# Half of the columns between two DFT stages kept in SBUF, moved by GpSimd-issued transfers, in a fused FFT filter and gated FFN kernel

## The chip, the cores and the metric

The kernel runs on one core of one Trainium2 chip. The metric is the device time of one execution in microseconds. Before the change three runs gave 1575.16 us in the median (1572.47 to 1579.84).

## The reference

`x` is 8 x 3136 x 256 in float32. Along the sequence of 3136 it is filtered in the frequency domain; the result goes through a feed-forward block with a gate.

```
X = np.fft.rfft(x, axis=1)
y = np.fft.irfft(X * (filt_r + 1j * filt_i), n=3136, axis=1)     # 8 x 3136 x 256
h = np.maximum(y @ w_in, 0)                                      # 256 -> 1024
conv = conv_w[0] * h[s - 1] + conv_w[1] * h[s] + conv_w[2] * h[s + 1]
out = (h * sigmoid(conv)) @ w_out                                # 1024 -> 256
```

The filter and the FFN weights come as constants too; the weights are 64-bit floats, which the kernel turns into float32 on VectorE.

## The kernel before, in words

The program has two phases. In the first, all eight batches go through the transform; in the second the FFN runs over chunks of 896 positions with TensorE full all the time, and the last stage of the transform of batches 1 to 7 is slipped in between. The change is in the first phase.

The length 3136 is split into 112 x 28. A batch then is 28 columns of 112 points (x 256 channels), worked through in 14 pairs. Each pair takes these steps:

- `first` (L317): TensorE multiplies two columns by `s1_sb` (matmuls at L321); ScalarE copies the result from PSUM into the tile `sa` (L309) and stores it to `a_dram` in DRAM (L315). Rows of a column are 112 outputs, which are 4 groups `r` of 28.
- load `a` (L304): the next stage needs, for an index `g`, the 4 groups of all 28 columns. So it needs the whole batch: 112 rows `(n r)` of `a_dram`, two values of `g` at a time. The way through DRAM is a transposition.
- `second` (L324): one matmul by `s2_sb` (L328; for the last pair L331 with `s2s_sb`).
- `filt` (L334): VectorE makes `u` and two halves of `v` from PSUM and the filter parts `t1_sb` and `t2_sb` (L340, L341, L342), GpSimd adds them to `z` (L344).
- `third` (L347): matmuls with `i1_sb` (L351), copied by ScalarE to `sb` (L309) and stored to `b_dram` (L315). The last stage later reads it as `br` (L199), multiplies by `m2_sb` (L216) and writes `y` (L146, L149).

One loop (L369) over `i` sets the order of the work on TensorE, VectorE, ScalarE and GpSimd by hand: the iteration `i` makes `first` of pair `i - 1`, and, `SKEW` = 18 iterations later, `second` of pair `m - 1`, `filt` of `m - 2` and `third` of `m - 4`, with `m = i - SKEW`. On TensorE a full iteration is thus `third`, `first`, `second`. Two kinds of small work are slipped into it: the conversion of weights (`convert_weights` L273, eight pieces of 11 steps each, one step in eight of nine iterations), and `copy_filter` (L251) on ScalarE, which copies the filter parts to the other partition half. From `done` = 118 on, the last stage of batch 0 runs in the loop as well (L408 to L414). SyncE's queue, which holds all loads, is not ordered by hand: a scheduler orders it. ScalarE's queue holds its own stores in order with its copies. Every transfer of SyncE and ScalarE signals through one of eight semaphores and waits for the transfer that used it before.

Buffers: eight tiles of `x`, five of `a`, four of `sa`, four of `sb`, five of PSUM `ps`, three of PSUM `pp`, three of `z`.

Of the kernel before, what the change touches and what calls it, by code (L numbers as in the profile page):

```python
# [9 lines left out]
F32 = mybir.dt.float32  # L10
# [28 lines left out]
def _dft_tables():  # L39
# [85 lines left out]
def tile_fft_filter_gated_ffn(  # L125
# [56 lines left out]
    a_dram = [dram.tile([N2, 112, D], F32, name=f"a_dram{b}") for b in range(B)]  # L182
# [44 lines left out]
    s1_sb = xp.tile([112, N2, 112], F32, name="s1_sb", bufs=1)  # L227
    with (
# [13 lines left out]
        t2_sb = fc.tile([120, G, D], F32, name="t2_sb")  # L242

        rows = {}

        def load_filter(c):
            sl = slice(4 * c, 4 * c + 4)
            for t, src in ((t1_sb, fr), (t2_sb, fi)):
                nc.sync.dma_start(out=t[0:64, sl], in_=src[:, sl])

        def copy_filter(c):  # L251
            sl = slice(4 * c, 4 * c + 4)
            nc.scalar.activation(t1_sb[64:120, sl], t1_sb[0:56, sl], AF.Copy)
            nc.scalar.activation(t2_sb[64:120, sl], t2_sb[0:56, sl], AF.Copy, scale=-1.0)
            if c == 6:
                nc.sync.dma_start(out=t1_sb[92:93, G - 1], in_=nyq)
# [3 lines left out]
        def load_weights(k):  # L260
            raws[k] = raw = cv.tile([128, 2, 512], I32, name="raw")
            for part, src in enumerate((w_in, w_out)):
                nc.sync.dma_start(out=raw[:, part], in_=src[:, 512 * k:512 * k + 512])

        def convert_conv():
            n = 3 * NF
            raw = cv.tile([128, 2, 512], I32, name="raw")
            nc.sync.dma_start(out=raw[:, 0, 0:2 * n], in_=conv_w)
            yield
            em = cv.tile([128, 2, 512], I32, name="em", bufs=1)  # L270
            yield from to_f32(cw.rearrange("p k f -> p (k f)"), raw[:, 0, 0:2 * n], em[:, 0, 0:n], em[:, 1, 0:n])

        def convert_weights():  # L273

            for k in range(8):
                raw = raws.pop(k)
                em = cv.tile([128, 2, 512], I32, name="em", bufs=1)
                ws = cv.tile([128, 2, 256], F32, name="ws")
                yield from to_f32(ws.rearrange("p t n -> p (t n)"), raw.rearrange("p t n -> p (t n)"), em[:, 0], em[:, 1])
                yield  # L280
                parts = [[t.rearrange("p a b -> p (a b)")[:, 256 * k:256 * k + 256] for t in w] for w in (wi, wo)]
# [6 lines left out]
                if k < 6:  # L288
                    load_weights(k + 2)
# [5 lines left out]
        def pool(kind):  # L295
            return xp if kind in ("x", "sa") else fp

        def load(kind, b, p):
            r = pool(kind).tile([112, 2, D], F32, name=kind, bufs=8 if kind == "x" else 5)
            if kind == "x":  # L300
                v = x[b].rearrange("(p n) d -> p n d", n=N2)
            else:
                v = a_dram[b].rearrange("n (r g) d -> (n r) g d", g=G)
            nc.sync.dma_start(out=r, in_=v[:, 2 * p:2 * p + 2])  # L304
            rows[kind, b, p] = r

        def store(kind, b, p, ps):
            st = pool(kind).tile([112, 2, D], F32, name=kind, bufs=4)
            nc.scalar.activation(st, ps, AF.Copy)  # L309
            sl = slice(2 * p, 2 * p + 2)  # L310
            if kind == "sa":
                v = a_dram[b][sl].rearrange("n p d -> p n d")
            else:
                v = b_dram[b].rearrange("n (r g) d -> (n r) g d", g=G)[:, sl]
            nc.scalar.dma_start(out=v, in_=st)  # L315
# [8 lines left out]
        def second(b, p):  # L324
            r = rows.pop(("a", b, p))
            pp = fps.tile([120, 2, D], F32, name="pp", bufs=3)
            if p < NP - 1:
                nc.tensor.matmul(pp, lhsT=s2_sb, rhs=r, start=True, stop=True)  # L328
            else:
                for j, m in ((0, s2_sb), (1, s2s_sb)):  # L330
                    nc.tensor.matmul(pp[:, j], lhsT=m, rhs=r[:, j], start=True, stop=True)  # L331
            psums[b, p] = pp

        def filt(b, p):  # L334
# [7 lines left out]
            nc.vector.tensor_mul(v[0:56], pp[64:120], t2_sb[64:120, sl])  # L342
# [14 lines left out]
        SKEW = NP + 4  # L357
        nc.sync.dma_start(out=s1_sb[:, 0:4], in_=s1[:, 0:4])
        load("x", 0, 0)
        load("x", 0, 1)  # L360
        for c in range(1, 4):
            nc.sync.dma_start(out=s1_sb[:, 4 * c:4 * c + 4], in_=s1[:, 4 * c:4 * c + 4])
            load("x", 0, 2 * c)
            load("x", 0, 2 * c + 1)
        csteps, wsteps = convert_conv(), convert_weights()
        done = NP * B + 6
        NI = max(NP * B + SKEW + 5, done + N2 // 2 + 3)
        with tc.manual_schedule(engines=COMPUTE):
            for i in range(NI):  # L369
# [5 lines left out]
                if 1 <= i < 4:  # L375
                    nc.sync.dma_start(out=s1_sb[:, 4 * i + 12:4 * i + 16], in_=s1[:, 4 * i + 12:4 * i + 16])
                if (bp := at(f + 7)) and i:
                    load("x", *bp)
                if bp := at(m + 3):
                    load("a", *bp)  # L380
                if i == 6:
                    nc.sync.dma_start(out=s2_sb, in_=s2[:, 0:120])
                    nc.sync.dma_start(out=s2s_sb, in_=s2s[:, 0:120])
# [9 lines left out]
                if bp := at(m - 1):  # L393
                    second(*bp)
                if pt is not None:
                    store("sb", *at(m - 4), pt)
                if pf is not None:
                    store("sa", *at(f - 1), pf)
# [5 lines left out]
                if i >= 22 and i % 9 != 8:  # L404
# [161 lines left out]
```

## Time and profile before

| | |
|---|---|
| profiled execution, span | 1573.9 us |
| runs, median | 1575.16 us |
| TensorE busy over the span | 1510.8 us (96%) |
| VectorE, ScalarE, GpSimd busy | 1280.7, 1192.6, 698.0 us |
| moved by DMA | 166.83 MB, HBM read 88.03, written 77.07 MB |
| DMA from GpSimd's queue | none |

The profile is of one execution. PE is TensorE's matmuls, PEld its weight loads, DVE VectorE, ACT ScalarE, POOL GpSimd, SP SyncE; a trailing q is an engine's issuing of transfers, which does not count as busy. In a group's row stand the line, the engine, the operation and its tiles, how many there were, the busy time in all and the mean of one in ns, and after the second bar how long the engine sat idle ahead of them and what ended that. In a row of windows each engine has its busy time and the number of its instructions, then follow the granted clock of TensorE, the share of the 16 DMA engines that was busy, and the rate.

### The profile page before, as it was taken

The page shows a single profiled execution, that of the slowest core. Times are in us where ns is not written, and L with a number is a line of the kernel's source. Part 1 is how long each engine was busy: PE and PEld are TensorE (multiplying, and loading weights), DVE is VectorE, ACT ScalarE, POOL GpSimd, SP SyncE. Part 2 cuts the span into 40 slices and gives each one's busy share as a digit, 9 for nine tenths or more (in the row PEclk, how much of TensorE's full clock was granted, in tenths as well). Part 3 has the DMA queues.
Part 4 walks back from the last instruction along what each step waited for, and adds up shares of the span by engine and source line. Part 5 has one row for each costly group of instructions (what it writes and reads, how often), then busy time and mean ns, then how long its engine had stood idle before and what let it go on. Part 6 is the DMA issues. An engine that isn't in the chain of part 4 may idle for free.

```text
span 1573.9 us, 26330 instructions
## 1 busy us (share of the span) xinstructions
PE 1510.8 (96%) x9424; PEld 1351.0 (86%) x9424; DVE 1280.7 (81%) x1965; ACT 1192.6 (76%) x2162; POOL 698.0 (44%) x624
## 2 busy tenths in 40 slices
PE   5699999998999999999999999999999999999998
PEld 4366666656999999999999999999999999999998
DVE  0487878897888888888888888888888888888887
ACT  3444444445988888888888888888888888888887
POOL 0255555562444444444444444444444444444444
PEclk8699999999999999999999999999999999999999
DMA  9999999984111011111111111111111111100001
GB/s 292 298 345 349 341 309 338 340 251 142 30 48 48 30 48 48 48 48 48 40 33 36 47 48 49 46 48 47 36 42 48 48 37 41 48 24 25 24 24 48
DMA packets 128278, 166.83 MB, mean 106 GB/s; under 512 B 10682, under 2 KB 87571, under 8 KB 128147
## 3 DMA queue, kind: packets, MB, share of 16 engines
q1 hardware_dynamic: 86931, 113.74, 23.1%
q10 hardware_dynamic: 41216, 51.39, 9.9%
q8 instruction: 75, 1.23, 0.3%
q14 instruction: 56, 0.46, 0.1%
HBM read 88.03 MB, written 77.07 MB: 105 GB/s over the span
## 4 chain that ended last, share of the span: by engine, by line
PE 83%; DMA 9%; DVE 4%; ACT 2%; issue 1%; ACTq 0%; POOL 0%; SPq 0%; DVEq 0%; POOLq 0%
PE ps_h L178 12%; PE ps_h L179 12%; PE ps_h L177 11%; PE po L473 11%; PE po L475 11%; PE po L474 11%; PE ps_h L216 5%; PE ps L321 4%; DMA x<-in_x 3%; PE ps L351 3%; PE pp L328 3%; DMA a<-a_dram 2%; DMA a_dram<-sa 2%; DVE y L149 1%; DVE v L341 1%
## 5 line engine op out<-in xcount | busy, mean ns | idle before, releaser
L152 POOL TENSOR_TENSOR g<-t,g 128x448 fp32r<-128x448 f32 x448 | 517.6, 1156 | 667.6 <-ACT g L146 265.8
L473 PE MATMUL po<-wo,g 128*128 128x256 f32 x1568 | 441.5, 282 | 0.0
L475 PE MATMUL po<-wo,g 128*128 128x256 f32 x1568 | 433.8, 277 | 0.0
L474 PE MATMUL po<-wo,g 128*128 128x256 f32 x1568 | 433.4, 276 | 0.0
L447 DVE SCALAR_TENSOR_TENSOR t<-ps_h,cw,t 128x448 f32<-128x448 f32 x448 | 305.5, 682 | 83.9 <-ACT t L442 73.3
L178 PE MATMUL ps_h<-y,wi 128*128 128x450 f32 x896 | 330.8, 369 | 4.2 <-DVE y L149 4.2
L177 PE MATMUL ps_h<-y,wi 128*128 128x450 f32 x896 | 329.2, 367 | 3.4 <-ACT y L146 2.1
L179 PE MATMUL ps_h<-y,wi 128*128 128x450 f32 x896 | 329.2, 367 | 0.0
L448 DVE SCALAR_TENSOR_TENSOR t<-ps_h,cw,t 128x448 f32<-128x448 f32 x448 | 306.4, 684 | 16.0
L442 ACT ACTIVATE t<-ps_h,cw 128x448 f32<-128x448 f32 x448 | 285.2, 637 | 42.1 <-ACT ps_h L440 0.7
L473 PEld LDWEIGHTS po<-wo,g 128*128 128x128 f32 x1568 | 294.7, 188 | 7.0
L474 PEld LDWEIGHTS po<-wo,g 128*128 128x128 f32 x1568 | 294.3, 188 | 5.7
L475 PEld LDWEIGHTS po<-wo,g 128*128 128x128 f32 x1568 | 294.4, 188 | 0.0
L440 ACT ACTIVATE ps_h<-ps_h 128x450 f32<-128x450 f32 x448 | 251.6, 562 | 32.5 <-PE ps_h L179 27.7
L453 DVE TENSOR_TENSOR t<-ps_h,t 128x448 f32<-128x448 f32 x448 | 275.1, 614 | 0.1
L452 ACT ACTIVATE t<-t 128x448 f32<-128x448 f32 x448 | 255.1, 569 | 12.2 <-DVE t L448 11.0
L146 ACT ACTIVATE g<-t 128x448 fp32r<-128x448 f32 x448 | 254.4, 568 | 0.2 <-DVE t L453 0.2
L344 POOL TENSOR_TENSOR z<-u,v 120x512 f32<-120x512 f32 x112 | 157.2, 1404 | 169.5 <-DVE v L342 144.8
L177 PEld LDWEIGHTS ps_h<-y,wi 128*128 128x128 f32 x896 | 170.4, 190 | 12.0 <-ACT y L146 3.3
L179 PEld LDWEIGHTS ps_h<-y,wi 128*128 128x128 f32 x896 | 168.6, 188 | 13.9
L178 PEld LDWEIGHTS ps_h<-y,wi 128*128 128x128 f32 x896 | 168.6, 188 | 13.5 <-DVE y L149 6.6
L149 DVE TENSOR_TENSOR y<-ps_h,y 128x448 fp32r<-128x448 f32 x98 | 103.1, 1052 | 76.7 <-ACT y L146 76.7
(51 smaller groups left out, 1447.5 us busy)
## 6 DMA issues: line engine op xcount, KB each, us to landing
x<-in_x SPq DMA_DIRECT2D x112, 224.0 KB, 4.6
a_dram<-sa ACTq DMA_DIRECT2D x112, 224.0 KB, 4.5
a<-a_dram SPq DMA_DIRECT2D x112, 224.0 KB, 4.7
b_dram<-sb ACTq DMA_DIRECT2D x112, 224.0 KB, 4.1
br<-b_dram SPq DMA_DIRECT2D x112, 224.0 KB, 2.6
out<-ot SPq DMA_DIRECT2D x27, 896.0 KB, 4.1
raw<-in_w_in SPq DMA_DIRECT2D x8, 256.0 KB, 4.6
raw<-in_w_out SPq DMA_DIRECT2D x8, 256.0 KB, 5.3
```

What stands on the lines that cost most here:

```text
L152: nc.gpsimd.tensor_tensor(out=dst, in0=src, in1=hi.bitcast(F32), op=ALU.subtract)
L177: nc.tensor.matmul(ps, lhsT=wh, rhs=rh, start=start, stop=False, **kw)
L178: nc.tensor.matmul(ps, lhsT=wh, rhs=rl, start=False, stop=False, **kw)
L179: nc.tensor.matmul(ps, lhsT=wl, rhs=rh, start=False, stop=stop, **kw)
L442: nc.scalar.activation(t, h[:, 1:SUB + 1], AF.Copy, scale=cw[:, 1, f:f + 1])
L447: nc.vector.scalar_tensor_tensor(out=t, in0=h[:, 0:SUB], scalar=cw[:, 0, f:f + 1], in1=t, op0=ALU.mult, op1=ALU.add)
L448: nc.vector.scalar_tensor_tensor(out=t, in0=h[:, 2:SUB + 2], scalar=cw[:, 2, f:f + 1], in1=t, op0=ALU.mult, op1=ALU.add)
L452: nc.scalar.activation(t, t, AF.Sigmoid)
L453: nc.vector.tensor_mul(t, h[:, 1:SUB + 1], t)
L473: nc.tensor.matmul(o, lhsT=gh[:, sl], rhs=wo[0][:, f], start=first, stop=False, skip_group_check=True)
L474: nc.tensor.matmul(o, lhsT=gh[:, sl], rhs=wo[1][:, f], start=False, stop=False, skip_group_check=True)
L475: nc.tensor.matmul(o, lhsT=gl[:, sl], rhs=wo[0][:, f], start=False, stop=last, skip_group_check=True)
```

## The change

Of each pair of columns, the even one no longer goes through DRAM. `store_a` writes only the odd column to `a_dram` (now 14 x 112 x 256 for a batch). One iteration later `turn` issues, on GpSimd's queue, a transfer that takes the even column of `sa` (112 rows of 1 KB) to four partitions `p`, `p + 14`, `p + 28`, `p + 42` of a whole-batch buffer `a_sb[b % 2]`, 28 KB in each. The odd columns are loaded into partitions 56 to 111 of it by `load_a`, 112 KB each, two a iteration in the first seven iterations of a batch, from iteration `m + 1` on. `second` reads the buffer. The rows of `s2` are put in the matching order.

To make room for two buffers of 28 KB per partition, other tiles shrink: seven tiles of `x`, three of `sb`; weight pieces of half the size (sixteen of them), two steps an iteration from `i` = 22; `ws` in one buffer; GpSimd's descriptor space at 4096 bytes. `fi` is loaded to partitions 64 to 127 and copied to 0 to 55, where the sign is now taken by VectorE: the third product is a scalar_tensor_tensor with -1.0. The filter is loaded in pieces of 128 KB, twice as many. `SKEW` goes from 18 to 16 and `done` from 118 to 116, so the loop has 133 iterations and not 135.

```diff
-        return np.concatenate([re, gap, im, -im, gap, re], 1)
+        rows = np.array([56 + 2 * (n - 1) + r if n % 2 else 14 * r + n // 2 for n in range(28) for r in range(4)])
...
-    a_dram = [dram.tile([N2, 112, D], F32, name=f"a_dram{b}") for b in range(B)]
+    a_dram = [dram.tile([N2 // 2, 112, D], F32, name=f"a_dram{b}") for b in range(B)]
...
+    a_sb = [xp.tile([112, G, D], F32, name="a_even", bufs=1)]
...
+        a_sb.append(fc.tile([112, G, D], F32, name="a_odd"))
...
-            for k in range(8):
+            for k in range(16):
...
+        def load_a(b, p):
+            v = a_dram[b].rearrange("n (r g) d -> (n r) g d", g=G)
+            nc.sync.dma_start(out=a_sb[b % 2][56:112, 2 * p:2 * p + 2], in_=v[:, 2 * p:2 * p + 2])
+
+        def store_a(b, p, ps):
+            st = xp.tile([112, 2, D], F32, name="sa", bufs=4)
+            nc.scalar.activation(st, ps, AF.Copy)
+            nc.scalar.dma_start(out=a_dram[b][p], in_=st[:, 1])
+            rows["sa", b, p] = st
+
+        def turn(b, p):
+            nc.gpsimd.dma_start(out=a_sb[b % 2][p:56:14], in_=rows.pop(("sa", b, p))[:, 0])
...
-            r = rows.pop(("a", b, p))
+            r = a_sb[b % 2][:, 2 * p:2 * p + 2]
...
-            nc.vector.tensor_mul(v[0:56], pp[64:120], t2_sb[64:120, sl])
+            nc.vector.scalar_tensor_tensor(out=v[0:56], in0=pp[64:120], scalar=-1.0, in1=t2_sb[64:120, sl], op0=ALU.mult, op1=ALU.mult)
...
-        SKEW = NP + 4
+        SKEW = NP + 2
...
-        done = NP * B + 6
+        done = NP * B + 4
...
-                if bp := at(m + 3):
-                    load("a", *bp)
...
+                if bp := at(m + 1):
+                    for p in (2 * bp[1], 2 * bp[1] + 1):
+                        if p < NP:
+                            load_a(bp[0], p)
...
                 if bp := at(m - 1):
                     second(*bp)
+                if bp := at(f - 2):
+                    turn(*bp)
...
-                if i >= 22 and i % 9 != 8:
+                if i >= 22:
+                    next(wsteps, None)
                     next(wsteps, None)
```

GpSimd's instructions around the first converted weights (`ws`, `wi`, `wo` are these, `z` is the sum of the filter), before:

```order
L174 TENSOR_TENSOR ws<-ws,em 128x512
L344 TENSOR_TENSOR z<-u,v_104 120x512
L344 TENSOR_TENSOR z<-u,v_103 120x512
L152 TENSOR_TENSOR wi_81<-ws,wi_80 128x256
L344 TENSOR_TENSOR z<-u,v_104 120x512
L152 TENSOR_TENSOR wo_83<-ws,wo_82 128x256
L344 TENSOR_TENSOR z<-u,v_103 120x512
```

The same place of GpSimd's queue after (`a_odd` is the buffer of batch 1, `sa` the tile that ScalarE filled):

```order
L177 TENSOR_TENSOR ws<-ws,em 128x256
L351 TENSOR_TENSOR z<-u,v_104 120x512
L317 DMA a_odd<-sa 4x28x256
L155 TENSOR_TENSOR wi_81<-ws,wi_80 128x128
L351 TENSOR_TENSOR z<-u,v_105 120x512
L317 DMA a_odd<-sa 4x28x256
L155 TENSOR_TENSOR wo_83<-ws,wo_82 128x128
L351 TENSOR_TENSOR z<-u,v_104 120x512
L317 DMA a_odd<-sa 4x28x256
```

Between any two sums now stands the issue of one transfer.

SyncE's queue at the start of the second stage of batch 1, before (`x` are inputs of `first`, `a` those of `second`):

```order
L304 DMA x<-in_x 112x512
L304 DMA a<-a_dram_58 112x512
L304 DMA x<-in_x 112x512
L304 DMA a<-a_dram_58 112x512
L304 DMA x<-in_x 112x512
L304 DMA a<-a_dram_58 112x512
```

SyncE's queue where the second stage of batch 3 starts, after:

```order
L303 DMA x<-in_x 112x512 x5
L308 DMA a_odd<-a_dram_60 56x512 x9
L303 DMA x<-in_x 112x512
L308 DMA a_odd<-a_dram_60 56x512 x5
L269 DMA raw<-in_w_in 128x256
L269 DMA raw<-in_w_out 128x256
L303 DMA x<-in_x 112x512 x5
```

The loads of the second stage stood one by one between those of `x`; now the fourteen of a batch stand in a block, and the `x` behind them wait in the queue until the first of the block may go.

More of the change, by code (lines that the diff above doesn't have):

```diff
@@ L104, in s2 @@
         re, im, gap = m[:, 0].reshape(112, 56), m[:, 1].reshape(112, 56), np.zeros((112, 8))
-        return np.concatenate([re, gap, im, -im, gap, re], 1)
+        rows = np.array([56 + 2 * (n - 1) + r if n % 2 else 14 * r + n // 2 for n in range(28) for r in range(4)])
+        out = np.zeros((112, 120))
+        out[rows] = np.concatenate([re, gap, im], 1)
+        return out
     i1 = i1.reshape(2, 56, G, 112)
@@ L241, in tile_fft_filter_gated_ffn @@
         t1_sb = fc.tile([120, G, D], F32, name="t1_sb")
-        t2_sb = fc.tile([120, G, D], F32, name="t2_sb")
+        t2_sb = fc.tile([128, G, D], F32, name="t2_sb")
+        a_sb.append(fc.tile([112, G, D], F32, name="a_odd"))
         rows = {}
         def load_filter(c):
-            sl = slice(4 * c, 4 * c + 4)
-            for t, src in ((t1_sb, fr), (t2_sb, fi)):
-                nc.sync.dma_start(out=t[0:64, sl], in_=src[:, sl])
+            for k in range(2):
+                sl = slice(4 * c + 2 * k, 4 * c + 2 * k + 2)
+                nc.sync.dma_start(out=t1_sb[0:64, sl], in_=fr[:, sl])
+                nc.sync.dma_start(out=t2_sb[64:128, sl], in_=fi[:, sl])
         def copy_filter(c):
@@ L287, in convert_weights @@
                     yield
[L288 removed]
+                if k < 14:
                     load_weights(k + 2)
@@ L293, in tile_fft_filter_gated_ffn, with load, store_b @@
         psums = {}
[L295 to L315, printed above, removed]
+        def load(b, p):
+            r = xp.tile([112, 2, D], F32, name="x", bufs=7)
+            nc.sync.dma_start(out=r, in_=x[b].rearrange("(p n) d -> p n d", n=N2)[:, 2 * p:2 * p + 2])
+            rows["x", b, p] = r
+        def load_a(b, p):
[3 more added lines that the diff above has]
+            st = xp.tile([112, 2, D], F32, name="sa", bufs=4)
+            nc.scalar.activation(st, ps, AF.Copy)
+            nc.scalar.dma_start(out=a_dram[b][p], in_=st[:, 1])
+            rows["sa", b, p] = st
+        def turn(b, p):
+            nc.gpsimd.dma_start(out=a_sb[b % 2][p:56:14], in_=rows.pop(("sa", b, p))[:, 0])
+        def store_b(b, p, ps):
+            st = fp.tile([112, 2, D], F32, name="sb", bufs=3)
+            nc.scalar.activation(st, ps, AF.Copy)
+            nc.scalar.dma_start(out=b_dram[b].rearrange("n (r g) d -> (n r) g d", g=G)[:, 2 * p:2 * p + 2], in_=st)
         def first(b, p):
@@ L355, in at @@
             return divmod(i, NP) if 0 <= i < NP * B else None
-        SKEW = NP + 4
+        SKEW = NP + 2
         nc.sync.dma_start(out=s1_sb[:, 0:4], in_=s1[:, 0:4])
-        load("x", 0, 0)
-        load("x", 0, 1)
-        for c in range(1, 4):
+        load(0, 0)
+        load(0, 1)
+        for c in range(1, 3):
             nc.sync.dma_start(out=s1_sb[:, 4 * c:4 * c + 4], in_=s1[:, 4 * c:4 * c + 4])
-            load("x", 0, 2 * c)
-            load("x", 0, 2 * c + 1)
+            load(0, 2 * c)
+            load(0, 2 * c + 1)
+        load(0, 6)
         csteps, wsteps = convert_conv(), convert_weights()
-        done = NP * B + 6
+        done = NP * B + 4
         NI = max(NP * B + SKEW + 5, done + N2 // 2 + 3)
@@ L394, in tile_fft_filter_gated_ffn @@
                     second(*bp)
+                if bp := at(f - 2):
+                    turn(*bp)
                 if pt is not None:
-                    store("sb", *at(m - 4), pt)
+                    store_b(*at(m - 4), pt)
                 if pf is not None:
-                    store("sa", *at(f - 1), pf)
+                    store_a(*at(f - 1), pf)
                 if 3 <= i < 16:
```

30 lines of the change are left out of this document (15 added, 15 removed).

## The prediction

> **What bounds the kernel now.** I read the page's slices first. In its 40 slices of 39.3 us each, the busy tenths of TensorE and of the DMA engines and the moved GB/s are these:
>
> ```profile
> PE   5699999998999999999999999999999999999998
> DMA  9999999984111011111111111111111111100001
> GB/s 292 298 345 349 341 309 338 340 251 142 30 48 48 30 48 48 48 48 48 40 33 36 47 48 49 46 48 47 36 42 48 48 37 41 48 24 25 24 24 48
> ```
>
> The transform is the first ten slices; there the DMA engines are full, later nearly idle. Everything that the change edits lies there. To place the stages I took three matmuls from the chain of waits and the timeline (start, duration): the first `second`, the last `first`, and the first of the last stage of batch 0.
>
> ```profile
> 55.94 2.06 PE pp L328 x2
> ...
> 324.25 1.03 PE L321 MATMUL ps<-x,s_sb 112*112 112x256 f32 x4
> ...
> 342.79 1.04 PE L216 MATMUL ps<-m_sb,br 112*128 112x112 f32 x8
> ```
>
> Cut there, the windows give each engine's busy time and count, the granted clock, the DMA share and GB/s:
>
> ```profile
> core 0: us, PE busy (x) PEld busy (x) DVE busy (x) ACT busy (x) POOL busy (x), PEclk, DMA share, GB/s
> 0.00:56.00 56.00, 29.87 (x89) 19.84 (x89) 5.30 (x13) 20.25 (x29) 4.04 (x10) 0.80 0.98 291
> ...
> 90.00:324.00 234.00, 220.48 (x827) 145.94 (x828) 192.28 (x289) 102.15 (x178) 132.46 (x103) 0.99 1.01 336
> 324.00:343.00 19.00, 15.78 (x55) 8.87 (x53) 18.32 (x28) 6.19 (x12) 12.23 (x9) 1.00 0.76 231
> 343.00:385.00 42.00, 36.36 (x192) 27.15 (x190) 37.51 (x51) 22.79 (x29) 18.63 (x20) 1.00 0.66 195
> 385.00:1573.00 1188.00, 1179.35 (x8176) 1130.95 (x8176) 1005.46 (x1553) 1024.20 (x1893) 518.60 (x476) 1.00 0.13 41
> ```
>
> So: a fill of 56 us (only `first`, DMA share 0.98), a steady stage to 324 us, a drain to 385, and 1189 us of FFN, which I leave as they are. The chain shows what paces the steady stage, in pieces of start, duration and place:
>
> ```profile
> 212.67 0.86 PE ps L321 x4
> 213.54 0.86 PE pp L328 x2
> 214.40 0.86 PE ps L351 x4
> ...
> 216.16 4.54 DMA x<-in_x
> 220.71 5.29 DMA a<-a_dram
> 226.49 0.61 ACT sb L309
> ```
>
> An iteration is 3 x 0.86 = 2.59 us of TensorE while nothing is late; now and then a transfer is. Sizes and landing times of the transfers:
>
> ```profile
> x<-in_x SPq DMA_DIRECT2D x112, 224.0 KB, 4.6
> a_dram<-sa ACTq DMA_DIRECT2D x112, 224.0 KB, 4.5
> a<-a_dram SPq DMA_DIRECT2D x112, 224.0 KB, 4.7
> b_dram<-sb ACTq DMA_DIRECT2D x112, 224.0 KB, 4.1
> br<-b_dram SPq DMA_DIRECT2D x112, 224.0 KB, 2.6
> raw<-in_w_in SPq DMA_DIRECT2D x8, 256.0 KB, 4.6
> t_sb<-in_fr SPq DMA_DIRECT2D x7, 256.0 KB, 5.4
> i_sb<-in_i SPq DMA_DIRECT2D x7, 210.0 KB, 5.2
> s_sb<-in_s SPq DMA_DIRECT2D x7, 196.0 KB, 4.3
> ```
>
> An iteration moves 4 x 224 KB = 917 kB, at 336 GB/s 2.73 us; weights (512 KB per 12.4 iterations, 42 kB each) add 0.13: 2.86 us. The stage makes 82 iterations (82 sums `z` in the rows below) in 234 us, 2.85 us each. DMA sets the pace now, a tenth above TensorE. The rows of VectorE and GpSimd in that window (count, busy us, mean ns, idle before):
>
> ```profile
> L344 POOL TENSOR_TENSOR z<-u,v 120x512 f32<-120x512 f32 x82 | 115.9, 1414 | 92.3 <-DVE v L342 77.5 <-PE pp L328 12.1 <-PE ps L321 2.4
> L342 DVE TENSOR_TENSOR v<-pp,t_sb 56x512 f32<-56x512 f32 x82 | 56.8, 693 | 2.4
> L340 DVE TENSOR_TENSOR u<-pp,t_sb 120x512 f32<-120x512 f32 x81 | 56.0, 692 | 35.9 <-PE pp L328 28.4 <-POOL z L344 5.2 <-issue 0.7
> L341 DVE TENSOR_TENSOR v<-pp,t_sb 56x512 f32<-56x512 f32 x81 | 55.4, 684 | 2.0
> L174 POOL TENSOR_TENSOR ws<-ws,em 128x512 f32<-128x512 f32 x7 | 8.9, 1267 | 0.0
> L152 POOL TENSOR_TENSOR wo<-ws,wo 128x256 fp32r<-128x256 f32 x7 | 5.1, 729 | 0.0
> L152 POOL TENSOR_TENSOR wi<-ws,wi 128x256 fp32r<-128x256 f32 x7 | 5.1, 728 | 11.2 <-ACT wi L146 11.2
> L172 DVE SCALAR_TENSOR_TENSOR em<-raw,em 128x512 f32<-128x512 uint32 x6 | 4.2, 693 | 0.2
> L162 DVE TENSOR_SCALAR em<-raw 128x512 int32<-128x512 int32 x7 | 3.0, 428 | 0.2
> ```
>
> **Steady stage, DMA.** Of 224 KB stored and 224 KB loaded per iteration, 112 KB of each go, and 112 KB of `turn` come: 784 KB = 803 kB, 2.39 us at 336 GB/s, with 48 kB of weights 2.53 us. Below TensorE's 2.59, so the most that is to be had from this is 2.85 - 2.59 = 0.26 us an iteration.
>
> **VectorE.** The scalar_tensor_tensor that replaces the third product costs the same: that form took 693 ns over as many columns (L172), the product 693. A half-size weight piece is seven operations of half the length; with three of 0.69 and four of 0.43 whole, at least 1.9 us per 5.5 iterations. 2.07 + 0.35 = 2.42 us: hidden under 2.59, with little to spare.
>
> **GpSimd.** An iteration is a sum, 1.41 us, and a share of the weights, (1.27 + 0.73 + 0.73) / 2 per 5.5 iterations = 0.25. New is the issue of `turn`, X. No transfer of before is issued by GpSimd, so I bound it: SyncE's issue of one is
>
> ```profile
> 199.82 0.31 SPq L304 DMA_DIRECT2D x<-in_x  x1
> ```
>
> 0.31 us; the upper end is a whole unhurried transfer, 2.6 us (`br`). GpSimd has to write out 112 rows in software where SyncE only hands them over, and its own shortest regular instruction is 0.73 us; I take 1.0, nearer to that row than to either end. At the low end TensorE paces (2.59 us); at the high end the pace would be 4.26 us, and how far towards it is weighed with the first rival. Then GpSimd needs 1.41 + 0.25 + 1.0 = 2.66 us, more than TensorE: it becomes the pace by a hair, and it has to be gap-free. Behind a `turn` in its queue wait the next sums, and `third` two iterations later waits for these. The Trainium skill (DMA: Bandwidth & Descriptors, Latency and other measured facts) puts the first byte of a GpSimd-issued transfer at about 1 us and of a SyncE or ScalarE one at 0.6; if the 0.4 between them were all of the extra work, X would be 0.7 and TensorE would stay the pace.
>
> **Batch boundaries.** Before, `a` was loaded four iterations ahead of its use; now the first `load_a` is issued two ahead, and it waits for the store of the batch's last column. Counted from the start of that column's iteration: `first` done at 1.7, copy and issue to about 2.7, landing 3 to 4.5 (between `br` and `sa`), issue 0.3, landing again 3 to 4.7: 9.0 to 12.2. `second` stands at 3 x 2.59 + 1.7 = 9.5. The last `turn` goes out an iteration after, behind its sum: at 2.6 + 2.1 + 1.4 + X = 7.1, landing 3 to 4.5, 10.1 to 11.6. So `second` is late by nothing to 2.7 us, and what stands behind in TensorE's and SyncE's queues (fourteen loads in a block, then `x`) shifts along; ScalarE's stores share the eight semaphores with that block. That ScalarE can be held by such a load shows in the waits (in total, times, longest):
>
> ```profile
> ACT sb L309 <- DMA a<-a_dram: 24.0, 13, 5.7
> ```
>
> I take 2.5 us for each of the boundaries, 2.5 / 14 = 0.18 us an iteration. Pace: 2.66 + 0.18 = 2.84 us.
>
> **Fill.** `second` now stands at iteration 17, behind all filter loads in SyncE's queue. Ahead of it go, as the queue stands now, in KB: 24 `x` 5376, `s1` 1372, filter 3584, `i1` 1470, the small tables about 180 by their shapes, weights 512, and 16.5 iterations of stores and turns 3696: 16,190 KB = 16.6 MB, at 291 GB/s 57 us. As late as before, but at iteration 17 and not 19.
>
> **Sum.** To the last `first`, 57 + 95 x 2.84 = 327 us (before 324). Drain: the last stage starts 5 and not 7 iterations after it. Those 19 us held 28 VectorE instructions, 24 of the filter and 4 of weights; the weights are done by iteration 110 now, so 5 x 2.2 = 11 us (2.07 of VectorE and its gaps): -8, and one boundary in it, +2.5. Total 3 - 5.5 = -2.5 us: 1571.4 for the span of 1573.9. The median of the runs is 1.3 above that span, so 1572.7: I say 1572. Gain or loss goes with the pace: 95 us for each us of it. Under 0.5% (8 us) a difference is about what the measurement can't tell.
>
> **Rivals.**
> *GpSimd sets the pace* (slower). Above X = 1.03 the sum turns positive; at X = 1.5, 1.41 + 0.25 + 1.5 = 3.16, with half the boundary loss hidden 3.25: 57 + 309 - 324 - 5.5 = +36, 1612; at 1.2, 2.86 and 2.95 to 3.04, +8 to +16. The high end of 2.6 us would make +132, 1707. For: a `turn` in each gap between sums, and the sums are at 1.41 already. Against: GpSimd sat idle 92 us before its 82 sums, 1.13 us each. Chance 0.30.
> *A turn is slow in landing.* Its destination has four rows of 28 KB. If only four of the sixteen engines carry it, each moves 28 KB where `sa` put 14 KB on each in 4.5 us; L could reach 7. ScalarE needs the tile again four iterations after its copy, so and the turn is issued an iteration after that, at 2.1 + 1.4 + 1.0 = 4.5 us of it, the copy at 2.0 of its own: with the pace P, 4P + 2.0 >= P + 4.5 + L, P >= (2.5 + L) / 3 = 3.17, 57 + 301 - 324 - 5.5 = +29, 1604; at L = 5 it is nothing. Chance 0.07. The Trainium skill (DMA: Bandwidth & Descriptors, Why a DMA increments its semaphore by 16 and not by 1) has the engines limited to the largest count up to 16 that divides both slowest dimensions, here 4; no transfer of this trace has such a shape.
> *All is hidden.* X at 0.7, landings near 2.6 us as on unhurried queues, boundaries without loss: P = 2.65, 57 + 252 - 324 - 8 = -23, 1552. For: the DMA engines would have 15% to spare. Against: four engines within a few per cent of one pace, in tight buffers. Chance 0.20.
> *Nothing relieved.* SBUF-to-SBUF bytes could cost DMA engines as much as the two halves that they replace: P stays 2.85, 1572 also. Chance 0.03.
>
> **How the numbers follow.** Forecast 0.40, most within 0.5% of 1575 (0.20), 0.13 better, 0.07 worse. Faster 0.13 + 0.20 = 0.33; same 0.20 + 0.02 (mild slow landing) + 0.03 = 0.25; slower 0.07 + 0.30 + 0.05 = 0.42. Range: down to 1550 (all hidden, 0.07 beyond), up to 1606 (X about 1.45; with slow landing 0.12 beyond). The forecast's own range is 1560 to 1584.
>
> **What would show it.** Right: 2.6 to 2.9 us between sums in the steady stage, DMA share under 0.95, GpSimd with next to no idle time, `second` late once in 14. Wrong: sums over 3 us apart with GpSimd's issues of more than 1.2 us between them; ScalarE waiting for `turn` at `sa`; a drain that is not shorter; a fill far from 57 us.

## The result, and the profile after

The changed kernel takes 1676.20 us in the median of four runs (1671.94 to 1682.61), the kernel before, run beside it, 1576.97 us (1572.47 to 1579.84). The ratio is 1.063, with a 95% interval of 1.060 to 1.066: slower by 99 us, where 1572 was forecast and 1606 was the upper end. The profiled execution of after has a span of 1680.6 us.

The slices of its page (40 of 42.0 us) already show where to look: the FFN is as before, the transform takes twelve slices and not ten, and the DMA engines are nearly full at two thirds of the rate.

```profile
PE   4387877887889999999999999999999999999998
DMA  9878888787631111111111111111101111100001
GB/s 224 194 207 242 223 227 230 225 239 209 182 109 29 50 45 34 45 50 50 45 45 45 34 45 45 50 45 50 45 29 45 50 45 49 46 29 23 23 23 45
```

To cut the time by stage I took from the timeline of TensorE the first `second`, which names what it waited for, of after and of before:

```profile
78.42 2.03 PE L335 MATMUL pp<-a_even,s_sb 112*120 112x512 f32 x2 [13.56 <-DMA a_even<-a_dram]
```

```profile
44.82 2.06 PE L328 MATMUL pp<-a,s_sb 112*120 112x512 f32 x2 [10.06 <-DMA a<-a_dram]
```

Before, this is at 44.8 and not at 55.9. The prediction took the first `second` that stood in the chain of waits for the first that ran. With cuts at the first `second`, the last `first` and the first matmul of the FFN, the windows of after and then of before are these (the columns as in the prediction's windows):

```profile
0.00:78.40 78.40, 25.27 (x68) 15.88 (x69) 1.16 (x7) 10.44 (x17) 11.76 (x23) 0.66 0.91 211
78.40:425.40 347.00, 277.92 (x950) 175.08 (x951) 282.57 (x396) 131.89 (x233) 207.36 (x236) 0.91 0.82 223
425.40:491.10 65.70, 53.28 (x231) 37.32 (x229) 48.40 (x66) 27.41 (x37) 25.95 (x26) 0.89 0.62 174
```

```profile
0.00:44.80 44.80, 23.43 (x76) 16.49 (x76) 1.16 (x7) 16.94 (x25) 1.51 (x8) 0.83 0.97 293
44.80:324.20 279.40, 256.08 (x930) 167.76 (x931) 218.50 (x328) 122.50 (x205) 147.25 (x113) 0.95 1.01 331
324.20:385.10 60.90, 51.94 (x243) 35.85 (x242) 55.64 (x79) 29.04 (x40) 30.67 (x28) 1.00 0.69 206
```

So 34 us more in the fill, 68 in the steady stage (95 iterations of 3.65 us, before 93 of 3.00), 5 in the drain. In the steady stage no engine is full: VectorE is busy 283 of 347 us, GpSimd 207, and DMA fell to 223 GB/s. The issue of a turn on GpSimd, and how long a turn takes to land, by the groups (84 to 424 us) and the page's list of DMA issues:

```profile
L317 POOL DMA_DIRECT2D a_odd<-sa x51 | 35.2, 691 | 29.4 <-ACT sa L312 29.1
L317 POOL DMA_DIRECT2D a_even<-sa x42 | 28.9, 688 | 24.2 <-ACT sa L312 24.1
```

```profile
a_even<-sa POOLq DMA_DIRECT2D x56, 112.0 KB, 6.5
a_odd<-sa POOLq DMA_DIRECT2D x56, 112.0 KB, 6.1
```

A turn costs GpSimd 0.69 us and lands after 6.1 to 6.5 us. The waits (84 to 424 us; total, times, longest) are spread over many pairs, with the transfers around `sa` and the late products of VectorE among them; for a turn itself ScalarE waits little, which is the last two lines, 8.3 us together:

```profile
POOL z L351 <- DVE v L349: 80.8, 45, 6.7
ACT sa L312 <- DMA a_even<-a_dram: 29.3, 3, 11.9
ACT sa L312 <- DMA x<-in_x: 17.6, 10, 6.7
PE pp L335 <- DMA a_even<-a_dram: 12.9, 2, 8.3
ACT sa L312 <- DMA a_even<-sa: 5.1, 3, 2.0
...
ACT sa L312 <- DMA a_odd<-sa: 3.2, 3, 1.3
```

VectorE's timeline shows the two conversion steps of an iteration: the first takes 0.29 or 0.45 us, the second is stretched, and the next `u` starts only behind it. Below it is what GpSimd does at these times.

```profile
250.54 0.29 DVE L173 TENSOR_SCALAR em<-ws 128x256 int32<-128x256 int32 x1
250.87 1.37 DVE L175 SCALAR_TENSOR_TENSOR em<-raw,em 128x256 f32<-128x256 uint32 x1
252.27 0.69 DVE L347 TENSOR_TENSOR u<-pp,t_sb 120x512 f32<-120x512 f32 x1
...
258.73 0.45 DVE L163 TENSOR_SCALAR em<-raw 128x256 int32<-128x256 int32 x1
259.09 2.26 DVE L165 TENSOR_SCALAR em<-raw 128x256 int32<-128x256 int32 x1
```

```profile
250.69 1.27 POOL L351 TENSOR_TENSOR z<-u,v 120x512 f32<-120x512 f32 x1 [2.33 <-DVE v L349]
...
259.10 0.47 POOL L155 TENSOR_TENSOR wi<-ws,wi 128x128 fp32r<-128x128 f32 x1
259.51 0.46 POOL L155 TENSOR_TENSOR wo<-ws,wo 128x128 fp32r<-128x128 f32 x1
259.93 1.27 POOL L351 TENSOR_TENSOR z<-u,v 120x512 f32<-120x512 f32 x1
```

And ScalarE's timeline in the fill shows copies that wait some 10 us each for a load of constants that they have nothing to do with. The likely reason is that the store ahead of them in the queue shares a semaphore with that load.

```profile
36.44 0.60 ACT L312 ACTIVATE sa<-ps 112x512 f32<-112x512 f32 x1 [9.96 <-DMA i_sb<-in_i]
...
48.39 0.60 ACT L312 ACTIVATE sa<-ps 112x512 f32<-112x512 f32 x1 [11.36 <-DMA t_sb<-in_fr]
```

That gave three theories. **A**: VectorE's conversion steps, two in a row under a sum of GpSimd. **B**: the order of SyncE's queue, which a scheduler makes, with the eight semaphores that SyncE and ScalarE share. **C**: a turn is carried by few of the sixteen DMA engines, and what crosses these is slowed.

### The profile page after: what moved, and what is told of

Its sections match the earlier page's. It is cut to its first block, busy times and chain, and to the rows that moved or that the text cites. A ratio compares the mean times of both kernels' runs of the same rounds, so it can differ in the third digit from the quotient of the medians.

```text
span 1680.6 us, 26750 instructions
## 1 busy us (share of the span) xinstructions
PE 1535.3 (91%) x9424; PEld 1358.8 (81%) x9424; DVE 1337.7 (80%) x2021; ACT 1193.5 (71%) x2178; POOL 763.6 (45%) x760
## 2 busy tenths in 40 slices
DMA packets 126999, 154.15 MB, mean 92 GB/s; under 512 B 22138, under 2 KB 90579, under 8 KB 126867
## 4 chain that ended last, share of the span: by engine, by line
PE 75%; DMA 13%; DVE 5%; issue 3%; ACT 1%; SPq 1%; POOL 1%; ACTq 0%; DVEq 0%; POOLq 0%
PE ps_h L181 11%; PE ps_h L182 11%; PE ps_h L180 11%; PE po L486 11%; PE po L488 10%; PE po L487 10%; PE ps_h L219 5%; DMA x<-in_x 4%; PE ps L328 2%; DMA a_dram<-sa 2%; PE ps L358 2%; PE pp L335 2%; DMA a_even<-a_dram 1%; DVE v L348 1%; DMA a_odd<-a_dram 1%
## 5 line engine op out<-in xcount | busy, mean ns | idle before, releaser
L312 ACT ACTIVATE sa<-ps 112x512 f32<-112x512 f32 x112 | 66.8, 597 | 195.6 <-DMA a_even<-a_dram 40.9
L351 POOL TENSOR_TENSOR z<-u,v 120x512 f32<-120x512 f32 x112 | 145.0, 1295 | 119.2 <-DVE v L349 114.4
```

## The experiments

Each is one run of one execution; the time of the kernel before beside it was 1575.8 to 1576.3 us, beside e5 to e8 1582.4. Four runs of the kernel before lay 7 us apart, so a difference of less than some 8 us between two runs tells nothing.

### A and B, each alone

**e1**: the second conversion step goes between VectorE's second and third product.

```diff
             nc.vector.tensor_mul(v[64:120], pp[0:56], t2_sb[0:56, sl])
+            if b * NP + p + SKEW + 2 >= 22:
+                next(wsteps, None)
...
                 if i >= 22:
                     next(wsteps, None)
-                    next(wsteps, None)
```

> The changed kernel, with the second of the two weight-conversion steps of an iteration moved: it stands between VectorE's second and third product of the filter, where GpSimd's sum has ended, and not right behind the first step. Theory A (VectorE's conversion steps are held by GpSimd's sum, which reads the same memory port): in the changed kernel the seven conversion operations took 88 us in all for sixteen half-size pieces, against 30.6 us before for eight whole pieces. With the step moved they fall to about 40 us, and the pace inside a batch from 3.2 us an iteration to 2.7 to 2.9: 30 to 45 us less than the changed kernel, about 1635 to 1645 us. Theory B (late transfers alone: the block of loads, the shared semaphores, the turns) expects less than 10 us of difference: 1668 us or more.

Measured: 1668.1 us. Steady stage 333 in place of 347 us, fill 78 as before the edit. The costliest conversion rows of after and of e1 (84 to 424 us):

```profile
L165 DVE TENSOR_SCALAR em<-raw 128x256 int32<-128x256 int32 x16 | 15.2, 952 | 0.2
L171 DVE SCALAR_TENSOR_TENSOR ws<-em 128x256 f32<-128x256 int32 x16 | 14.9, 930 | 1.1
```

```profile
L165 DVE TENSOR_SCALAR em<-raw 128x256 int32<-128x256 int32 x16 | 6.9, 434 | 0.4
L171 DVE SCALAR_TENSOR_TENSOR ws<-em 128x256 f32<-128x256 int32 x16 | 6.8, 426 | 0.5
```

The same operations take half the time at another place in the iteration; all seven together fell from 88 to 50 us. The time is 8 us below the median of after and 4 below its lowest run: VectorE's conversion is a small cost at most, and not the main one. In the timelines above, the step of 1.37 us began inside a sum of GpSimd and ended 0.28 us behind it, and the one of 2.26 us lasted through two weight operations and a sum and ended 0.15 us behind them. The Trainium skill (SBUF — State Buffer, SBUF: two separate sides) has GpSimd and some operations of VectorE, those with two SBUF inputs or in a two-port mode, take turns at a shared port, one of them blocked for a whole instruction of the other. The 1.37 and 2.26 us agree with that, against 0.29 to 0.45 for the first of a pair; in which mode an operation ran, no run here shows.

**e2**: SyncE's queue keeps the order in which the program is written.

```diff
-        with tc.manual_schedule(engines=COMPUTE):
+        with tc.manual_schedule(engines=FIRST):
...
+FIRST = COMPUTE | {mybir.EngineType.SP}
```

> The changed kernel with SyncE's queue in the order of the code in the loop: filter loads two iterations apart, at most two loads of the second stage after each load of x, instead of the scheduler's blocks. Theory B (the order of SyncE's queue holds the loads of x and, through the shared semaphores, ScalarE's stores): the first second-stage matmul moves from 78.4 us back to 56 to 62, and the TensorE gaps at the six batch boundaries, 42 us in all, fall to 15 to 25: 35 to 50 us less, 1626 to 1641 us. Theory A (VectorE held by GpSimd) expects only the fill to move: about 15 to 20 us less, or nothing. Theory C (the turns: four engines, landing after 6.2 us) expects the boundaries to stay as they are and the fill to stay above 70 us.

Measured: 1650.6 us, span 1648.7. The steady stage stayed at 346 us; the first `second` came at 53.5 in place of 78.4:

```profile
53.48 2.03 PE L335 MATMUL pp<-a_even,s_sb 112*120 112x512 f32 x2 [7.92 <-DMA a_odd<-sa]
```

TensorE's gaps of over 1.5 us in the steady stage did not shrink as B expected: 49 us in all, 45 in after. So B is the fill, and 26 us against the median of after; it isn't the pace.

### C: what a turn costs

**e3** leaves out the turns (the even halves are set to zero once), **e4** sends 56 rows of 2 KB to 56 partitions in place of 112 rows to four.

```diff
-                if bp := at(f - 2):
-                    turn(*bp)
```

```diff
-            nc.gpsimd.dma_start(out=a_sb[b % 2][p:56:14], in_=rows.pop(("sa", b, p))[:, 0])
+            nc.gpsimd.dma_start(out=a_sb[b % 2][0:56, 2 * p:2 * p + 2], in_=rows.pop(("sa", b, p))[0:56])
```

> The changed kernel without the moves of the even columns: the even half of the whole-batch buffers is set to zero once by GpSimd, so half of the columns is left out of the second stage; the rest of the work is as in the changed kernel. Theory C (the turns are what costs, as GpSimd's issues of 0.69 us and as traffic on four engines): the kernel falls to or below the time of before, 60 to 110 us less, 1565 to 1615 us, with landings near 4 us. Theory B expects 15 to 35 us less (112 KB less per iteration, no wait at the tile sa), boundaries remain. Theory A expects 5 to 15 us less: the sum still holds the conversion steps.

> The changed kernel with another shape of the turn, as many bytes: 56 rows of 2 KB of the tile sa go to 56 partitions of the buffer instead of 112 rows of 1 KB to four partitions, so the data of the even half is not what the second stage needs. Theory C, in the form that four engines carry a turn: its landing falls from 6.2 to 3 to 4.5 us and the kernel is 30 to 60 us faster, 1615 to 1645 us. Theories A and B expect less than 10 us of difference, a little of it from the boundary, since a second-stage matmul here needs one turn and not all fourteen.

Measured: e3 1590.0 us, e4 1614.4 us, its turns landing in 4.5 us. In both the scheduler also gave SyncE another order (first `second` at 41 and 47 us), so they hold part of B and don't separate it. Hence the next three with the order fixed.

**e5** is e2 with e1's edit. **e6** is e5 with e4's wide turn. **e7** is e5 with the true turn as four transfers of one partition each:

```diff
-            nc.gpsimd.dma_start(out=a_sb[b % 2][p:56:14], in_=rows.pop(("sa", b, p))[:, 0])
+            st = rows.pop(("sa", b, p))
+            for r in range(4):
+                nc.gpsimd.dma_start(out=a_sb[b % 2][p + 14 * r:p + 14 * r + 1], in_=st[28 * r:28 * r + 28, 0])
```

> SyncE's queue by hand and the second conversion step moved, both edits of the first two runs in one kernel; the turns are as in the changed kernel. Theory C (turns that four engines carry, landing late, hold the tile sa, the boundary and the loads behind them) expects that this gains next to nothing over the queue by hand alone, which took 1648.7 us of span: 1630 to 1648, with turns still landing after more than 6 us and gaps of about 4 us at each boundary. Theory A (VectorE held by GpSimd is the main limit) expects the pace inside a batch to fall to 2.7 us: 1605 to 1615.

> The same with the turn in the wide shape (56 rows of 2 KB to 56 partitions, so the even half does not hold what the second stage needs). Theory C expects turns to land within 4.5 us, and with VectorE relieved as well a pace of 2.6 to 2.8 us: 1560 to 1580 us, the time of before or less. If the bytes of the turns, and not their shape, are what costs, it stays at 1610 or above.

> The same with the true turn in four transfers from GpSimd, each from 28 rows to one partition, whose outer sizes of 28 allow fourteen engines and not four. Theory C expects the landing of these transfers to fall below 5 us; but at about 0.45 us an issue GpSimd then needs 1.3 + 0.25 + 1.8 = 3.35 us an iteration and sets the pace: 57 + 95 x 3.4 to the last first-stage matmul and 60 of drain, 1620 to 1640 us, with GpSimd never idle. If the landing stays above 6 us although GpSimd has time, the four engines were not the cause.

Measured: e5 1650.8, e6 1588.5, e7 1676.5 us. The windows of the steady stage and the sums in them, of e5 and then of e6:

```profile
90.00:380.00 290.00, 235.67 (x810) 152.05 (x809) 213.61 (x343) 108.79 (x198) 179.86 (x206) 0.89 0.86 241
...
L353 POOL TENSOR_TENSOR z<-u,v 120x512 f32<-120x512 f32 x81 | 105.4, 1302 | 81.6 <-DVE v L351 63.0 <-PE ps L328 10.3 <-PE pp L335 5.4
```

```profile
90.00:320.00 230.00, 207.03 (x761) 136.26 (x760) 201.19 (x321) 99.12 (x183) 155.40 (x193) 0.96 0.94 288
...
L353 POOL TENSOR_TENSOR z<-u,v 120x512 f32<-120x512 f32 x75 | 98.8, 1317 | 71.0 <-DVE v L351 61.6 <-PE pp L335 4.1 <-PE ps L360 2.9
```

290 / 81 = 3.58 us an iteration against 230 / 75 = 3.07, with the same bytes from the same issuer: the shape of the turn is worth 62 us, and DMA moves 288 GB/s in place of 241. Two things limit this pair. A `second` of e6 needs one turn and one of e5 all fourteen, and e6 stayed above the 1560 to 1580 us that C expected. Against e2, e1's edit gave e5 nothing that these runs can tell, so A is hidden while C lasts. e7 missed: its four issues cost GpSimd 4 x 0.51 us, and it is busy 285 of 310 us in the window below, so that GpSimd itself set the pace, 310 / 81 = 3.83.

```profile
90.00:400.00 310.00, 240.96 (x824) 149.22 (x823) 233.68 (x351) 112.58 (x203) 284.96 (x452) 0.94 0.85 233
...
L355 POOL TENSOR_TENSOR z<-u,v 120x512 f32<-120x512 f32 x81 | 104.0, 1284 | 20.4 <-DVE v L353 17.2 <-PE pp L337 2.7
```

**e8** puts A alone into the kernel before: half-size pieces, two steps in each iteration.

```diff
-            for k in range(8):
+            for k in range(16):
...
-                if i >= 22 and i % 9 != 8:
+                if i >= 22:
+                    next(wsteps, None)
                     next(wsteps, None)
```

> The kernel before with one part of the change alone: weight pieces of half the size, two conversion steps an iteration from iteration 22. Theory A expects the conversion operations to take over 75 us for the sixteen pieces here too (30.6 us before for the eight whole ones), since the sum of GpSimd starts with the first of the two steps, and VectorE to need 2.07 + 1.0 us or more an iteration: 15 to 35 us slower than before, 1590 to 1612 us. If the turns in GpSimd's queue are what held VectorE, the operations stay below 45 us and the time within 8 us of before.

Measured: 1592.0 us, 10 above the kernel before beside it, less than expected. The conversion took some 78 us in place of 31.

### Which property of the shape

**e9** has a wide turn over 51 partitions, **e10** is e6 with two of the seven conversion operations, **e11** and **e12** are e5 with the turn issued by ScalarE and by SyncE.

```diff
-            nc.gpsimd.dma_start(out=a_sb[b % 2][0:56, 2 * p:2 * p + 2], in_=rows.pop(("sa", b, p))[0:56])
+            n = slice(0, 412)
+            nc.gpsimd.dma_start(out=a_sb[b % 2][0:51, 2 * p:2 * p + 2].rearrange("q g d -> q (g d)")[:, n], in_=rows.pop(("sa", b, p))[0:51].rearrange("q g d -> q (g d)")[:, n])
```

```diff
-                yield from to_f32(ws.rearrange("p t n -> p (t n)"), raw.rearrange("p t n -> p (t n)"), em[:, 0], em[:, 1])
...
+                nc.vector.tensor_scalar(em[:, 0], pairs[:, :, 1], 3, 0x3FFFFFF8, op0=ALU.logical_shift_left, op1=ALU.bitwise_and)
...
+                nc.vector.scalar_tensor_tensor(out=flat, in0=pairs[:, :, 0].bitcast(U32), scalar=2.0**-52, in1=em[:, 0].bitcast(F32), op0=ALU.mult, op1=ALU.mult)
```

```diff
-            nc.gpsimd.dma_start(out=a_sb[b % 2][p:56:14], in_=rows.pop(("sa", b, p))[:, 0])
+            nc.scalar.dma_start(out=a_sb[b % 2][p:56:14], in_=rows.pop(("sa", b, p))[:, 0])
```

> The kernel of the run with the wide turn (56 partitions, 14 engines, 1588.5 us), with the turn cut to 51 partitions of 1648 bytes: 84 KB in place of 112, which by the count that divides 51 goes over three engines, 28 KB on each, as much as each of the four has in the true turn. The destination stays wide (51 partitions). The even halves hold zeros and wrong values: only the time counts. If few engines with 28 KB each are what makes a turn late (theory C, engines), it lands in 6 us or more, the boundaries show gaps again and the time is 1630 to 1665. If what makes it late is that all of it goes into four single partitions (C, partitions), it lands in under 5 us, with less to move than the wide turn, and the time is 1575 to 1595.

> The kernel of the run with the wide turn (1588.5 us), with two in place of seven VectorE operations for each half piece of weights; five are left out, so the weights hold wrong values and only the time counts. If VectorE with its conversion steps is what is left to pace the first phase once turns land early (theory A), its conversion goes from some 50 us to some 15 and the steady stage loses 25 to 35 us: 1553 to 1565. If something else paces it (GpSimd, the order at the boundaries, the transfers: B and C), little is gained: 1578 to 1590.

> The kernel with SyncE's queue by hand and the second conversion step moved (1650.8 us), with the true turn issued by ScalarE in place of GpSimd. If the carrying by four engines belongs to the shape (four rows of 28 KB) whoever issues it, it still lands in about 6 us and the boundaries keep their gaps: 1635 to 1665, or more where ScalarE's shared semaphores are held longer. If it belongs to GpSimd's software queue, it lands in 4 to 5 us and the time goes towards that of the wide turn: 1585 to 1610.

> The same with the turn issued by SyncE, in the order by hand, behind the loads of the same iteration. By the shape theory about 1635 to 1670 with landing near 6 us; by the theory of the software queue 1585 to 1610 with landing of 4 to 5 us. Either way a turn that waits for its copy on ScalarE holds the loads behind it on SyncE, which I put at 0 to 20 us.

Measured: e9 1580.5 us, landing 4.4. That was in the range of "single partitions", but the premise fell: the trace's records of single packets (100 to 300 us) have up to twelve of that queue at once, and more than four in a fifth of the time that any runs. A turn there is 13 packets of three rows and 12 of one, which fits thirteen engines with up to four rows each. So more than three engines carried it, and it tells nothing of few engines. The Trainium skill (DMA: Bandwidth & Descriptors, Why a DMA increments its semaphore by 16 and not by 1) names the exception that I passed over, that some GpSimd-issued copies go by 16 engines where the count of partitions does not divide. e10 1585.4 us, though VectorE in 90 to 320 us went from 201 to 168 us busy: what is left in e6 isn't VectorE either. e11 1664.0 us, 300 / 84 sums = 3.57 us an iteration: the shape is slow with another issuer too, which speaks against GpSimd's issuing and its descriptor space as the cause. It isn't a clean case, as ScalarE's turns also take part in the eight semaphores. The packets of e11 and e12 also count the engines. Each of the 224 stores of e5 closes with 16 packets of four bytes (3584 on ScalarE's queue), and the 112 turns add 448 of them in e11, and 448 on SyncE's queue in e12: 4 a turn, which fits one for each engine that carried a part. e12 1719.6 us, beyond its range; that turns on SyncE hold the loads behind them is the likely reason, and not shown.

**e13** to **e16** were to settle few engines against single partitions. e13 and e14 are e7 with two of the four transfers on ScalarE and on SyncE. e15 and e16 are e5 with the turn going to DRAM, so that no partition is written by it; the four blocks of 28 rows lie apart in e15, so that the shape keeps its outer four, and one behind the other in e16.

```diff
-                nc.gpsimd.dma_start(out=a_sb[b % 2][p + 14 * r:p + 14 * r + 1], in_=st[28 * r:28 * r + 28, 0])
+                (nc.gpsimd if r < 2 else nc.scalar).dma_start(out=a_sb[b % 2][p + 14 * r:p + 14 * r + 1], in_=st[28 * r:28 * r + 28, 0])
```

```diff
+    e_dram = [dram.tile([14, 4, 29, D], F32, name=f"e_dram{b}") for b in range(2)]
...
-            nc.gpsimd.dma_start(out=a_sb[b % 2][p:56:14], in_=rows.pop(("sa", b, p))[:, 0])
+            nc.gpsimd.dma_start(out=e_dram[b % 2][p][:, 0:28], in_=rows.pop(("sa", b, p))[:, 0])
```

(e16 has 28 for 29 and no `[:, 0:28]`.)

> The kernel with SyncE's queue by hand and the second conversion step moved (1650.8 us), with the true turn as four transfers of one partition (28 rows, 28 KB), two issued by GpSimd and two by ScalarE. The destinations are still single partitions, but each transfer goes over more than four engines, and GpSimd's issuing costs 2 x 0.5 us and not 2.0: 1.3 + 0.25 + 1.0 = 2.6 us an iteration. If four engines with 28 KB each are the cause, the pace goes from 3.6 towards that of the wide turn, 3.1 us: 1590 to 1615. If writing to single partitions is the cause, it stays near 3.6: 1635 to 1665. ScalarE's two issues may cost up to 10 us either way.

> The same with the second two of the four transfers on SyncE. By few engines 1590 to 1615, by single partitions 1635 to 1665, plus what SyncE's queue loses in waiting for the copy of ScalarE, 0 to 50 us (one turn on SyncE was 56 us slower than on ScalarE).

> The kernel with SyncE's queue by hand and the second conversion step moved (1650.8 us), with the turn going from the same rows to a scratch in DRAM whose four blocks of 28 rows don't follow on each other, so that it has the four rows of 28 KB of the true turn and goes over four engines, but into no partition at all. The even halves hold zeros: only the time counts. If four engines are the cause: landing of 6 us or more, pace near 3.5, 1625 to 1660. If single partitions are the cause: landing under 5.5, pace near 3.1, 1585 to 1605.

> The same with the four blocks following on each other, so that the 112 rows go over sixteen engines. Both theories: 1585 to 1605, pace near 3.1. If this is as slow as the run before, it is neither, but a cost of a transfer that GpSimd issues to 112 rows.

Measured: e15 1625.1, e16 1573.1 us. Windows and sums of e15, then of e16:

```profile
90.00:340.00 250.00, 208.42 (x743) 133.56 (x741) 196.56 (x318) 97.76 (x178) 164.13 (x187) 0.92 0.88 257
...
L356 POOL TENSOR_TENSOR z<-u,v 120x512 f32<-120x512 f32 x74 | 97.1, 1313 | 69.9 <-DVE v L354 50.7 <-PE ps L331 10.1 <-PE ps L363 5.4
```

```profile
90.00:340.00 250.00, 234.19 (x870) 155.33 (x869) 222.05 (x364) 108.89 (x203) 180.54 (x218) 0.97 0.92 291
...
L356 POOL TENSOR_TENSOR z<-u,v 120x512 f32<-120x512 f32 x89 | 116.5, 1309 | 66.9 <-DVE v L354 57.0 <-PE ps L363 5.6 <-PE pp L338 3.2
```

Same source, bytes, issuer and DRAM as destination: 3.38 against 2.81 us an iteration, 52 us in all; e16 came out below the 1585 to 1605 us that both theories gave it. The landing, of e15 and then of e16:

```profile
e_dram<-sa POOLq DMA_DIRECT2D x112, 112.0 KB, 6.2
```

```profile
e_dram<-sa POOLq DMA_DIRECT2D x112, 112.0 KB, 4.2
```

In the records of packets (100 to 300 us, packets of over 16 bytes), four or fewer of the turn's queue run at once in 95% of the time that any runs in e15 and in after, though turns overlap at times; in e16 it is 71%, and up to fourteen run. With the 4 closing packets of e11 and e12 this points to four engines, and no single partition is needed for the loss. One difference remains beside it: a turn is 28 packets of 4 KB and 84 of 16 bytes in e15 and 32 of 3 to 4 KB in e16. The small ones took 0.011 us each, and e5 and e6 both have 28 of 4 KB; but no run changes them alone.

Nor is it the turn that is waited for: the only wait on it in this window of e15 is the first line below, and `second` doesn't read it there. What is lost is lost by the other transfers, and more than half of it at the batch boundaries, as the waits of TensorE for the loads of `a` in the same window show:

```profile
ACT sa L315 <- DMA e_dram<-sa: 1.8, 1, 1.8
...
PE pp L338 <- DMA a_odd<-a_dram: 17.3, 3, 7.4
...
PE pp L338 <- DMA a_even<-a_dram: 13.3, 2, 6.8
```

From the first `second` to the last `first`, TensorE's gaps of over 1.5 us sum to 42 us in e15, 35 of them in six gaps a batch apart, and to 13 in e16 (55 in e5, 16 in e6). Without these gaps an iteration takes 2.96 us in e15 and 2.82 in e16. So the 3.38 us are not an even pace: 28 of the 52 us are these gaps.

Are they always the same four? The queue's line on e15's page says no:

```profile
q0 software_dynamic: 14336, 13.00, 3.5%
```

3.5% of 16 engines' 1623 us are 909 us for 112 turns, 8.1 us each. The window's 74 turns would fill 600 of four engines' 1000 us; the rest of the share, (0.88 x 4000 - 600) / 4000 = 0.73, would come on top if the other transfers are spread evenly: 1.33. It doesn't fit, so the four change from turn to turn. The page of the Trainium skill cited above has them move on in turn for GpSimd's transfers; which engines, no run here shows. The reading that is left: a turn piles 28 KB on four engines for a while, and each `x`, `sb` or `a` that goes over all of them is as late as its last part. The packets bear out the direction: ScalarE's stores take 1.4 us from the first to the last of their 16 closing packets in e15 and 1.1 in e16 (mean over 90 to 340 us, sixteen at a time in order of time). How that becomes gaps of 4 to 7 us at the boundaries is not shown.

e13 and e14 missed on both theories: 1743.4 and 1734.6 us. They spread the bytes (14 closing packets a transfer in place of 4) and took the load off GpSimd, and put two more transfers an iteration on the eight semaphores that ScalarE and SyncE share. That this is what made them slow was not tried alone, and so they decide nothing between few engines and single partitions. e13's waits of ScalarE (90 to 340 us):

```profile
ACT sb L323 <- DMA a_dram<-sa: 74.1, 33, 3.5
...
ACT sb L323 <- DMA a_even<-sa: 14.3, 3, 4.9
```

## Why the prediction was wrong

In its own steps, with spans: 1680.6 measured against 1571.4.

- **"784 KB = 803 kB, 2.39 us at 336 GB/s".** This step of the steady stage failed. It counted bytes and took it that all sixteen engines share them evenly. The bytes are right (154.15 MB against 166.83 for the whole program), the rate is 223 GB/s. e5 to e6 (62 us) and e15 to e16 (52 us) put the cause at the shape of the turn, and the packets at four engines carrying it. e16's 2.81 us an iteration lie beside the forecast's 2.84, but by luck: the forecast had GpSimd pace it, and there GpSimd sat idle 66.9 us ahead of 89 sums.
- **The rival "a turn is slow in landing"** had the four engines and named the page, with a chance of 0.07 and 1604 us. Its landing of up to 7 us was nearly right (6.1 to 6.5). Its mechanism was not: it let the turn act only through the reuse of `sa`, which costs 8 us in after, and not through the transfers of the other queues. The rule of the Trainium skill was the best evidence there was, and the chance given to it far too small.
- **Fill, 57 us; "as late as before".** The base was misread: 55.94 was a later `second`, the first was at 44.8. Costing the bytes ahead of it at 291 GB/s then gave 57, where 78.4 was measured at 211. e2 gets 53.5 by SyncE's order alone, so 25 us of it come from the scheduler's order: filter loads ahead of `x` and, as ScalarE's timeline suggests, stores behind shared semaphores. Most of the other 9 goes with the shape of the turn (51.9 in e15, 44.1 in e16). The prediction named both the filter loads and the eight semaphores, and priced the second at nothing here.
- **X = 1.0.** Mis-sized, on the safe side: 0.69. The estimate from the first-byte figures of the Trainium skill (DMA: Bandwidth & Descriptors, Latency and other measured facts) was 0.7. GpSimd at 1.30 + 0.25 + 0.69 = 2.24 us was not the pace of after, so the leading forecast and its largest rival (0.30) argued about a cost that wasn't there.
- **VectorE, "at least 1.9 us" for a piece.** The lower bound was used as the value: 88.1 / 16 = 5.5 us. A step after a step falls under GpSimd's sum. Alone it costs some 10 us (e8, one run), and with SyncE's order fixed it is hidden behind the turns (e5 against e2).
- **Boundaries, 2.5 us each.** In after, TensorE's gaps over 1.5 us sum to 45 us in the steady stage, most near the six boundaries. In e6, with wide turns, such gaps sum to 16 us, 2.7 for each boundary, in e16 to 13. So the estimate is near for a chain whose transfers land early; the rest goes with the turn's shape again. 28 of the 52 us between e15 and e16 came out here.
- **Drain, -5.5.** It went from 60.9 to 65.7 us. It is 59.6 in e2, so SyncE's order has to do with it; why was not tried further.

By the spans in a row: the order of SyncE's queue 32 us (1680.6 to 1648.7; after's profiled execution is the slowest of its four, and by the median it is 26), the turn's shape 62 (to 1586.7), conversion 3 (to 1583.3), and 9 are left over before. The last two are within what single runs can tell, as the kernel before was itself 7 us slower beside e6 than beside e10. Order matters in such a row: A was worth at most 8 to 15 at its start and nothing that can be told in the middle.

The expected gain was small in any case: e16, whose turns go evenly, ran at 1573.1 beside 1576.3, which single runs can't tell apart. None of the runs that do the whole work is faster than before.

Still open: by how much a write into single partitions adds to few engines (e5 and e15 differ by 26 us, 20 of it against the kernel before beside them, but `second` doesn't wait for the turn in e15), which engines carry it, and why the boundaries lose so much.

## What to carry to other kernels

Ask of a transfer not only how many bytes it has but over how many DMA engines its shape spreads them: an outer dimension of four, on 112 KB of some 800 an iteration, took 12 to 16% off the rate of all queues together (e16 to e15, e6 to e5), though little waited for the transfer itself. Ask too which transfers follow on each other with nothing to do meanwhile: at such places lateness turns into idle time. Read a stage's start from the timeline, not from the chain of waits, which shows only what ended last. And where a queue is left to a scheduler, read its order in the fill too: loads that moved ahead delayed the start by 25 us here.

## What the runs showed of the hardware

- A transfer's shape also sets its issue time on GpSimd: 0.69 us for 112 rows in four blocks (after, e15), 0.54 for the same 112 rows in a row (e16), 0.52 for 56 rows of 2 KB (e6), 0.51 for 28 rows (e7).
- A turn of four blocks closes with 4 packets of four bytes on ScalarE's and SyncE's queues (e11, e12), a transfer of 28 rows with 14 (e13, e14), a store of 112 rows with 16.
- A VectorE conversion operation on 128x256 took 0.29 to 0.45 us, or up to 2.26, by whether GpSimd's operations were running.
- After a long wait TensorE is slow for some us: the matmuls behind the stall of 13.56 us took 2.03 and 1.91 us where the usual group takes 1.03, and the granted clock was 0.50 from 78.4 to 82.0 us. Behind a wait of 4.16 us it was 0.56 (346.1 to 350.0), behind one of 2.27 us it stayed at 1.00 (125.3 to 129.0). A stall so costs more than its length: an estimate from the stage's granted clock is (1 - 0.91) x 347 = 31 us in after against (1 - 0.95) x 279 = 14 before.
